# Fused soft-capped attention and spectral mixing: scores of the first channel slot in two visits, its weight splits and sums reordered, one copy moved in the first mixing slot

## The chip, the cores and the metric

The kernel runs on 1 core of one Trainium2 chip. The metric is the device time of one execution in microseconds (us). Before the change it is 856.89 us, the median of 3 runs (856.53 to 857.65).

## The reference

The kernel computes attention with a soft cap on the scores, and then a mixing stage on its output. All inputs are float32; the batch is 8, with 12 heads, 448 positions and 64 features per head, so the model width is 768.

```python
def _attn_ref(q, k, v, cap):
    scores = (1.0 / np.sqrt(q.shape[-1])) * np.matmul(q, k.transpose(0, 1, 3, 2))
    scores = cap * np.tanh(scores / cap)
    scores = scores - np.max(scores, axis=-1, keepdims=True)
    attn = np.exp(scores)
    attn = attn / (np.sum(attn, axis=-1, keepdims=True) + 1e-09)
    return np.matmul(attn, v)

def _moe_ref(x, w_theta, w_tok_r, w_tok_i, w_ch):
    theta = x @ w_theta
    zr, zi = x * np.cos(theta), x * np.sin(theta)
    y = np.einsum('ts,bsd->btd', w_tok_r, zr) + np.einsum('ts,bsd->btd', w_tok_i, zi)
    u = x + y
    return u + np.maximum(u @ w_ch, 0.0)
```

The cap is 30. The kernel holds two programs, one of them for caps above 64 (`general`); only the other one runs here.

## The kernel before

**Slots.** Attention goes in 24 slots of 4 heads (two pairs, k = 2s and 2s + 1); three slots make one batch. The mixing stage of a batch lags: slot LEAD = 4 does the theta products of batch 0, slot 5 its token mixing, slot 6 its channel products, slot 7 theta of batch 1, slot 8 its mixing, and so on in threes. So slot 6 is the first channel slot. It also splits most of the channel weights, which happens once.

**Order.** Nothing is scheduled by a planner. `pipeline` (L735) walks a script of words per slot (L704 to L733), and every word issues its instructions at once; each engine and each DMA queue works in the order in which it got them, and waits in that order. So a word's place in the script sets its place in the queue of every engine that it uses.

**The words that matter.** `S0` to `S3` are the score products of one slot (L333): S0 the first two row chunks of the first pair; S1 its third chunk and, ahead of it, the remainders of both pairs (four pairs of products, two side by side); S2 and S3 the three chunks of the second pair. `t0` to `t3` are the tanhs that read them (L384, on ScalarE), `e0` to `e3` the exps (L422), `a0a` to `a1b` the additions of the exps (L440, on VectorE). `V0`, `W`, `Vr` are the products with v of the slot before, `Rb` the sums of its exps over the rows (L491), `cV0` and `cV1` the copies of its output (L486), `I` the inversion of its sums (L538), which transposes the sums (`turn`, L526), takes the reciprocal, transposes again and sends it by four DMAs on the SP queue to the tiles bc; `N` and `N-` multiply the output by bc (L561, VectorE). `Pa1`, `Pb1`, `Pa0`, `Pb0` split the raw q and k of a pair into a high part (a cast on ScalarE at first) and a low part (VectorE) (L305, L312). `u0` to `u5`, `Xh`, `Yh`, `Yl` split the inputs of the channel and theta products the same way (L569). `C0` to `C5` are the channel products (18 products each), `c0` to `c5` their results (VectorE, then a store on SP), `T0` to `T5` the theta products.

**Channel weights.** They come as float64 words in 12 half blocks, ch0a to ch5b. `:@ch3b` loads one, by two DMAs of 384 KB on the POOL queue (L187, L188); `:*ch3b` scales it on ScalarE (L153); `:0ch3b` and `:1ch3b` are four instructions on VectorE (L197 to L201); `:2ch3b` is a cast of the high part on ScalarE (L203) and the low part on VectorE (L204). C3 needs ch3a in its first half and ch3b in its second.

**Rooms.** Tiles of the large and of the small kind live in lists of rooms (L48). A take gets the first free room, and the new tile's first writer waits for the last users of the old one. By these lists ch3b goes into the room of ch2a, ch4a into that of ch2b, ch4b into that of ch3a and ch5a into that of ch3b, before and after.

**Two forms of scores.** Slots from HALVES on have the scores of S0 and S1 in two tiles of two banks each (s0, s1), S2 and S3 in four banks that all other products share, and `once` (L284) is true for them: half tanhs, a third chunk in s1, other rooms for the second pair's split k, the sums turned directly behind their products into the first tile of S1 (L523), cV1 on VectorE (L488). Slots below HALVES have one tile of four banks that S0, S1 and S2 take in turn, and tanhs of a whole tile. Slot 6 is of the second kind before the change:

```python
HALVES = LEAD + 3                                   # L43
def once(s):                                        # L284
    return LEAD + 2 < s < NS
if k + 1 < 2 * NS:                                  # L330, in prep_k
    load_raw(k + 1, 1, k % 2 == 0 and by_scalar(k) and k > 2 * LEAD + 8)
elif word == "I":                                   # L779, in run
    if done:
        invert(k)
```

Of the kernel before, what the change touches and what calls it, by code (L numbers as in the profile page):

```python
# [28 lines left out]
LEAD = 4  # L29
# [10 lines left out]

FOLD = (0, 1, 2)

HALVES = LEAD + 3  # L43

FILL = {"branch": 10, "S0": 2, "t0": 8, "t1": 4}

# [34 lines left out]
def softcap_attn_then_spectral_mix(ctx, tc, qk2, v, cap, w_theta, w_tok, w_ch, outT):  # L81
# [9 lines left out]
    NS = B * NP2  # L91
# [190 lines left out]
            state["scores"] = state["scope"].enter_context(tc.tile_pool(name=f"ps{general}{s}", bufs=1, space=bass.MemoryType.PSUM))  # L282

    def once(s):  # L284
        return LEAD + 2 < s < NS

    def load_raw(k, part, last=False):
        t = raw[k, part] = small.take([P, S], F32, f"{'qk'[part]}{k}", None, int(part == 0 and once(k // 2) and (k // 2 - LEAD) % NP2 == 2), last)
# [23 lines left out]
    def prep_k(k, early=False):  # L312

        if 2 * WHOLE <= k < 2 * NS:
            t = raw[k, 1]
            if once(k // 2) and k % 2:
                if (k, "rooms") not in Q:
                    Q[k, "rooms"] = [small.take([P, S], F32R, f"k{k}{part}") for part in "hl"]
                rooms = iter(Q[k, "rooms"])
                Q[k, "k"] = halves(t[:, :REST], [P, REST], lambda shape, dtype, name: next(rooms)[:, :REST], f"k{k}", by_scalar(k))  # L320
            else:
                Q[k, "k"] = halves(t[:, :REST], [P, REST], lambda shape, dtype, name: wk.tile(shape, dtype, tag=f"k{name[-1]}", name=name, bufs=1), f"k{k}", by_scalar(k))
            if k % 2 == 0:
                Q[k, "r"] = wk.tile([P, S - REST], F32, tag="kr", name=f"r{k}", bufs=1)
                nc.vector.tensor_copy(Q[k, "r"], t[:, REST:])
            if early:
                Q[k, "early"] = True
            else:
                small.give(raw.pop((k, 1)))
            if k + 1 < 2 * NS:  # L330
                load_raw(k + 1, 1, k % 2 == 0 and by_scalar(k) and k > 2 * LEAD + 8)

    def scores(s, n):  # L333
        if once(s) and n >= 2:
            t = spt[s, n] = [psM.tile([P, 512], F32, tag="m", name=f"s{s}_{n}{h}") for h in range(2)]
            if n == 3:
                two = spt[s, "u"] = state["scores"].tile([P, 2, 512], F32, tag="s1", name=f"s{s}_u")
                chunk(s, (1, 2), [two[:, h] for h in range(2)])
            chunk(s, (1, n - 2), t)
        elif n == 3 and not once(s) and s not in (1, LEAD + 1):  # L340
            t = spt[s, n] = [psM.tile([P, 512], F32, tag="m", name=f"s{s}_{n}{h}") for h in range(2)]
            chunk(s, (1, 2), t)
        else:
            two = spt[s, n] = state.pop("two", None) if once(s) and n == 1 else None
            if not two:
                two = spt[s, n] = halves_of(s, n)
            for u, what in sorted(enumerate(BURSTS[n]), key=lambda at: at[1] is not None):
                chunk(s, what, [two[0][u][:, h] for h in range(2)])
        k = 2 * s + n // 2
        if n in ((1, 3) if s else (1, 2)) and s < WHOLE:  # L350
            for part in range(2):
                small.give(raw.pop((k, part)))
        elif s >= WHOLE and n % 2:
            for t in Q.pop((k, "q")) + (Q.pop((k, "rooms")) if (k, "rooms") in Q else []):
                small.give(t)
            if n == 1:
                for i in range(2):
                    small.give(raw.pop((k + i, 0)))
                if Q.pop((k + 1, "early"), False):
                    small.give(raw.pop((k + 1, 1)))  # L360
                if k + 2 < 2 * NS:
                    for i in range(2, 4):
                        load_raw(k + i, 0, once(s) and (s - LEAD) % NP2 == 2)

# [332 lines left out]
    def chan_out(b, m):  # L697
# [21 lines left out]
        " T3 Pa0 Pb0 q1 y3 e2 e3 d3 sc1 T4 y4 T5 y5 a1a a1b r2 r3 f2 f3 D1 d4 d5",  # L719
        LEAD + 1: "S0 t0 Vr V0 Ra h0a l0a h0b l0b W h1a Rb :@ch0b cV0 cV1 sc2 Pa1 S1 Pb1 q0 t1 v M0a l1a r4 h1b M0b r5 l1b f4 f5 D2 e0 h2a M1a l2a m0 :#ch0b :0ch0b e1 :1ch0b M1b h2b l2b I :2ch0b :@ch1a"  # L720
        " S2 t2 M2a h3a l3a a0a M2b h3b l3b :@ch1b m1 M3a h4a l4a :*ch1a :0ch1a M3b h4b l4b a0b e2 m2 :1ch1a S3 q1 t3 M4a h5a l5a :2ch1a :@ch2a m3 M4b"
        " h5b l5b Pa0 Pb0 :*ch1b :0ch1b a1a u0 u1 e3 :1ch1b M5a :2ch1b :@ch2b m4 u2 M5b a1b m5 u3 :*ch2a :0ch2a u4 :@ch3a",
        LEAD + 2: "S0 t0 :1ch2a :2ch2a :@ch3b V0 u5 e0 :*ch2b :0ch2b W Ra Rb Vr cV0 cV1 v :1ch2b :2ch2b :@ch4a :*ch3a :0ch3a Pa1 S1 Pb1 q0 t1 :1ch3a :2ch3a :@ch4b :*ch3b C0 I c0 :0ch3b :1ch3b a0a e1 :2ch3b :@ch5a :*ch4a C1 :0ch4a :@ch5b"
        " S2 S3 t2 :1ch4a :2ch4a :*ch4b t3 c1 :0ch4b a0b C2 :*ch5a :1ch4b :2ch4b e2 :0ch5a :*ch5b C3 c2 :1ch5a :2ch5a :0ch5b :1ch5b :2ch5b a1a Pa0 Pb0 q1 N- c3 C4 e3 a1b c4 Xh0 Xh1 Xh2 Xh3 C5 c5",
        LEAD + 3: "Pa1 S0 t0 Pb1* V0 e0 N- Yh4 Yh5 W Ra Rb Vr cV0 S1 Yl0 Yl1 Yl2 cV1 t1 S2 S3 Yl3 Yl4 Yl5 v w0 q0 I w1 a0a q1 t2 e1 a0b Pa0 Pb0 Pa3 T0 y0 t3 d0 N T1 y1 Pb3* d1 F0 sc0 T2 y2 r0 r1 f0 f1 D0"
        " T3 y3 d2 d3 e2 e3 sc1 a1a a1b F1 T4 T5 r2 r3",
        LEAD + 4: "S0 t0 y4 y5 V0 f2 W Ra Rb f3 D1 h0a h0b h1a Vr cV0 S1 cV1 d4 t1a S2 S3 t2 l0a d5 l0b I l1a sc2b M0a h1b M0b r4 l1b r5 h2a M1a t3a f4 l2a h2b f5 D2 m0 l2b M1b h3a w1 t1b N e0"
        " l3a M2a h3b l3b a0a m1 M2b e1 t3b a0b M3a h4a l4a M3b h4b l4b h5a l5a e2 m2 F0 M4a h5b a1a l5b e3 Pa0 Pb0 m3 M4b v q1 a1b M5a m4 M5b F1 w3 m5",
        NS: "u0 u1 Vr V0 u2 u3 u4 u5 W cV0 cV1 Ra Rb I C0 c0 X0 X1 C1 c1 X2 X3 C2 c2 N X4 X5 T0+ y0+ d0+ T1+ y1+ d1+ sc0+ T2+ r0+ r1+ f0+ f1+ D0+ y2+ d2+ T3+"
            " y3+ d3+ sc1+ T4+ r2+ r3+ f2+ f3+ y4+ d4+ T5+ D1+ y5+ d5+ h0a+ l0a+ h0b+ l0b+ sc2+ C3 c3 r4+ r5+ f4+ f5+ D2+ C4 h1a+ l1a+ c4 C5 c5",  # L730
# [4 lines left out]
    def pipeline(general):  # L735
        state["general"] = general
        nc.scalar.activation(curve, quarter, AF.Tanh)
        def run(s, b, word):
            if word.endswith("+"):
                b, word = b + 1, word[:-1]  # L740
# [6 lines left out]
            if word == "S0>":  # L747
                scores(s + 1, 0)
            elif name in ("S", "t", "e"):
                if live:  # L750
                    {"S": scores, "t": tanh, "e": exp}[name](s, i, *word[2:])
            elif not name:
                if live:
                    add(s, i, half)
            elif word in ("Vr^", "V0^"):
                if word == "V0^":
                    av(s, 0)
                else:
                    av_rest(s, (0,) if general else (0, 1))
                if word == "V0^" or not general:  # L760
                    used(s, word[:2])
            elif word in ("Vr", "V0", "W"):
                if done:
                    if word == "W" and ("a", k, 1) not in acc_of and k < LEAD:
                        av_rest(k, (1,))
                        used(k, "Vr")
                    if word == "Vr":
                        av_last(k) if ("a", k, 0) in acc_of else av_rest(k)
                    else:
                        av(k, 0 if word == "V0" else 1)  # L770
                    used(k, word)
            elif name == "cV":
                if done:
                    av_out(k, i)
            elif name == "R":
                if done:
                    sums(k, word)
                    used(k, word)
            elif word == "I":  # L779
                if done:  # L780
                    invert(k)
            elif word in ("N", "N-"):
                if done:
                    norm(k - len(word) + 1)
            elif word == "v":
                if live:
                    load_v(s)
            elif name == "q":
                for part in range(2):
                    if s + 1 < WHOLE or s + 1 == WHOLE and (i, part) != (1, 1):  # L790
                        load_raw(2 * s + 2 + i, part)
            elif word in ("Pa1", "Pa3"):
                prep_q(2 * s + int(word[2]))
            elif word in ("Pb1", "Pb1*", "Pb3*"):
                prep_k(2 * s + int(word[2]), "*" in word)
            elif word == "Pa0":
                prep_q(2 * s + 2)
            elif word == "Pb0":
                prep_k(2 * s + 2)
            elif name == "F":  # L800
                if live and folded(s):
                    fold(s, i)
            elif name == "w":
                weights(WEIGHTS.get((s, i), ""))
            elif name in ("u", "uh", "ul"):
                split_x(b, i, "us", name[1:] or "hl")
            elif name in ("X", "Xh"):
                if b + 1 < B:
                    split_x(b + 1, i, "xs", name[1:] or "hl")
            elif name in ("Y", "Yh", "Yl"):  # L810
                split_x(b, i, "xs", name[1:] or "hl")
            elif name in ("h", "l", "M", "sc"):
                {"h": z_high, "l": z_low, "M": mix, "sc": sincos}[name](b, i, half)
            else:
                {"T": theta, "y": turns, "d": reduce, "r": rotate, "f": flip, "D": carry, "E": carry_end, "m": mix_out, "C": chan,
                 "c": chan_out}[name](b, i)
# [73 lines left out]
```

## Time and profile before

| | |
|---|---|
| time, median of 3 | 856.89 us |
| time of the profiled execution | 856.52 us |
| its span, first to last instruction | 854.6 us |
| TensorE matmul busy | 847.7 us, 99% of the span |
| VectorE, ScalarE, GpSimd busy | 719.2, 580.3 and 116.6 us |
| granted TensorE clock, mean | 0.999 |

The profiled execution is 0.37 us under the median. Times in the trace count from the first instruction of the span. Products on TensorE overlap, so its speed is read from the distance of two starts, not from the busy time. An instruction's own duration includes an overlap with the next one too, of about a tenth of a us.

Slot 6 begins at 138.29 us with S0, slot 7 at 172.24 us, slot 8 at 205.80 us.

### The profile page before, as it was taken

How to read it: one execution, taken by the hardware profiler on the slowest of the kernel's cores; microseconds unless marked ns; L12 is line 12 of the kernel's file. 1: busy time of each engine (PE TensorE's matmuls, PEld its weight loads, DVE VectorE, ACT ScalarE, POOL GpSimd, SP SyncE). 2: the span in 40 equal slices, each digit the busy share in tenths (PEclk: the TensorE clock that was granted, in tenths of full speed). 3: DMA queues.
4: the chain of work that ended last, by engine and by line, in shares of the span. 5: the costliest groups of instructions: out<-in, count | busy, mean ns of one | idle time of the engine just before them, and what ended most of it. 6: DMA issues, size and time to landing. Idle time of an engine off the chain costs nothing.

```text
span 854.6 us, 13331 instructions
## 1 busy us (share of the span) xinstructions
PE 847.7 (99%) x4756; PEld 646.3 (76%) x4756; DVE 719.2 (84%) x1164; ACT 580.3 (68%) x736; POOL 116.6 (14%) x244
## 2 busy tenths in 40 slices
PE   9999999999999999999999999999999999999997
PEld 5335676867978779779787787797787877979996
DVE  5988979999989799879998798897988979876741
ACT  6898987789873777827867478655787377824420
POOL 1121242201300031000310013000130003200300
PEclk9999999999999999999999999999999999999999
DMA  8686275741433324322423414144142332411401
GB/s 317 197 300 229 71 233 199 261 130 43 130 90 96 97 79 117 98 97 65 131 76 97 130 58 121 50 119 130 44 130 74 99 97 63 111 44 33 141 13 57
DMA packets 51693, 99.74 MB, mean 117 GB/s; under 512 B 11233, under 2 KB 42209, under 8 KB 51617
## 3 DMA queue, kind: packets, MB, share of 16 engines
q1 hardware_dynamic: 38880, 58.81, 22.3%
q0 software_dynamic: 9568, 29.89, 11.5%
q10 hardware_dynamic: 3168, 10.09, 3.9%
q8 instruction: 39, 0.64, 0.3%
q14 instruction: 38, 0.30, 0.1%
HBM read 54.72 MB, written 11.01 MB: 77 GB/s over the span
## 4 chain that ended last, share of the span: by engine, by line
PE 96%; ACT 2%; DVE 1%; issue 0%; ACTq 0%; POOL 0%; POOLq 0%
PE s L379 13%; PE a L483 13%; PE mx L684 8%; PE mx L686 8%; PE mx L685 8%; PE th L583 7%; PE ch L583 7%; PE ch L584 7%; PE th L584 7%; PE ch L585 7%; PE th L585 7%; PE a L477 2%; PE r L521 2%; PE s_u L379 1%; ACT p L405 1%; PE fill L130 1%
## 5 line engine op out<-in xcount | busy, mean ns | idle before, releaser
L653 POOL DMA_DIRECT2D t<-g_row x160 | 78.9, 501 | 528.6 <-ACT z L607 379.0
L684 PE MATMUL mx<-wtk_h,zh 128*128 128x448 f32 x336 | 123.7, 368 | 0.0
L686 PE MATMUL mx<-wtk_h,zl 128*128 128x448 f32 x336 | 122.9, 366 | 0.1
L685 PE MATMUL mx<-wtk_l,zh 128*128 128x448 f32 x336 | 122.8, 366 | 0.0
L425 ACT ACTIVATE p<-p,singles 128x1792 f32<-128x1792 f32 (+1 forms) x76 | 117.4, 1554 | 1.6 <-PE a L483 0.6
L583 PE MATMUL th<-xs,wth_h 128*128 128x448 f32 x288 | 106.1, 368 | 0.0
L583 PE MATMUL ch<-us,wch_h 128*128 128x448 f32 x288 | 105.9, 368 | 0.0
L584 PE MATMUL ch<-us,wch_h 128*128 128x448 f32 x288 | 105.9, 368 | 0.0
L584 PE MATMUL th<-xs,wth_h 128*128 128x448 f32 x288 | 105.5, 366 | 0.0
L585 PE MATMUL th<-xs,wth_l 128*128 128x448 f32 x288 | 105.5, 366 | 0.0
L585 PE MATMUL ch<-us,wch_l 128*128 128x448 f32 x288 | 105.4, 366 | 0.0
L483 PE MATMUL a<-p,v 128*64 128x448 f32 x492 | 101.8, 545 | 0.0
L411 ACT ACTIVATE p<-s,singles 128x896 f32<-128x896 f32 x34 | 32.4, 1004 | 91.2 <-PE s L379 91.2
L483 PEld LDWEIGHTS a<-p,v 128*64 128x64 f32 x492 | 32.9, 136 | 56.5 <-issue 51.9
L684 PEld LDWEIGHTS mx<-wtk_h,zh 128*128 128x128 f32 x336 | 63.1, 188 | 9.0 <-issue 2.5
L667 ACT CAST zh<-t 128x512 fp32r<-128x512 f32 x88 | 47.3, 563 | 29.9 <-PE mx L685 13.0
L686 PEld LDWEIGHTS mx<-wtk_h,zl 128*128 128x128 f32 x336 | 63.1, 188 | 5.8 <-DVE zl L674 0.6
L685 PEld LDWEIGHTS mx<-wtk_l,zh 128*128 128x128 f32 x336 | 63.1, 188 | 5.0
L674 DVE TENSOR_TENSOR zl<-t,zh 128x512 fp32r<-128x512 f32 x88 | 52.7, 611 | 12.2 <-ACT zh L667 11.1
L583 PEld LDWEIGHTS th<-xs,wth_h 128*128 128x128 f32 x288 | 54.0, 188 | 7.8 <-ACT p L408 1.9
L583 PEld LDWEIGHTS ch<-us,wch_h 128*128 128x128 f32 x288 | 54.0, 188 | 7.1 <-ACT p L408 1.6
L584 PEld LDWEIGHTS th<-xs,wth_h 128*128 128x128 f32 x288 | 54.0, 188 | 4.9 <-DVE xs L576 0.2
(718 smaller groups left out, 1707.6 us busy)
## 6 DMA issues: line engine op xcount, KB each, us to landing
v<-in_v ACTq DMA_DIRECT2D x22, 448.0 KB, 3.8
bc<-ri SPq DMA_DIRECT2D x88, 112.0 KB, 2.8
t<-g_row SPq DMA_DIRECT2D x160, 56.0 KB, 2.4
t<-g_row POOLq DMA_DIRECT2D x160, 56.0 KB, 2.2
q<-in_qk SPq DMA_DIRECT2D x39, 224.0 KB, 3.3
k<-in_qk SPq DMA_DIRECT2D x39, 224.0 KB, 3.7
out_dram<-x SPq DMA_DIRECT2D x34, 224.0 KB, 1.9
x_row<-in_qk SPq DMA_DIRECT2D x18, 224.0 KB, 2.8
```

Source lines behind the costliest of these rows:

```text
L379: nc.tensor.matmul(out[h][rows, :S], kk[half], qq[half], start=m == 0, stop=m == len(products) - 1)
L425: nc.scalar.activation(pp, pp, AF.Exp, scale=cap_sb)
L483: nc.tensor.matmul(acc_of["a", s, i][h * D : (h + 1) * D, :S], vt[s][:, 6 * i + 3 * h + c, :], U[s, (i, c)][:, h, :], start=first and c == ...
L583: nc.tensor.matmul(acc[:, :S], wh[:, j, ms], t[:, 0, :], start=j == 0, stop=False)
L584: nc.tensor.matmul(acc[:, :S], wh[:, j, ms], t[:, 1, :], start=False, stop=False)
L585: nc.tensor.matmul(acc[:, :S], wl[:, j, ms], t[:, 0, :], start=False, stop=j == NJ - 1)
L653: queue.dma_start(t[32 * m : 32 * m + 32, d * S : (d + 1) * S], f[32 * d : 32 * d + 32, m * S : (m + 1) * S])
L667: nc.scalar.copy(zh.rearrange("p c (d x) -> p c d x", x=32), tokens(b, j)[:, c0:c1])
L674: nc.vector.tensor_tensor(zl, tokens(b, j)[:, c0:c1], zh.bitcast(F32), op=ALU.subtract)
L684: nc.tensor.matmul(acc[:, :S], zh, wtk_h[:, c, :], start=c == 0, stop=False)
L685: nc.tensor.matmul(acc[:, :S], zh, wtk_l[:, c, :], start=False, stop=False)
L686: nc.tensor.matmul(acc[:, :S], zl, wtk_h[:, c, :], start=False, stop=c == NC2 - 1)
```

## The change

The bound HALVES and `once` move from slot 7 to slot 6, so slot 6 gets the second form of scores. Its script is rewritten: S2 and S3 follow S1, so TensorE does all scores of the slot before C0 (they make up two visits with S0, around the products with v); q13 and k13 are split at the start of the slot; t1 and t2 stand ahead of the casts and scales of weights from ch2a on; the sums are inverted behind the last weight split (`I-`, in the program that runs here; the other program keeps `I^` at the old place). The first instruction word of ch2a moves from slot 5 to slot 6. The load of k14 moves from prep_k to the end of S1. In slot 8 the word `h1a`, a cast of tokens on ScalarE (L667), moves from behind `h0b` to behind `t2`.

```diff
-HALVES = LEAD + 3
+HALVES = LEAD + 2
...
     def once(s):
-        return LEAD + 2 < s < NS
+        return LEAD + 1 < s < NS
...
-            if k + 1 < 2 * NS:
+            if k + 1 < 2 * NS and k != 2 * HALVES + 1:
                 load_raw(k + 1, 1, k % 2 == 0 and by_scalar(k) and k > 2 * LEAD + 8)
...
                 if k + 2 < 2 * NS:
+                    if s == HALVES:
+                        load_raw(k + 2, 1)
                     for i in range(2, 4):
...
-        " h5b l5b Pa0 Pb0 :*ch1b :0ch1b a1a u0 u1 e3 :1ch1b M5a :2ch1b :@ch2b m4 u2 M5b a1b m5 u3 :*ch2a :0ch2a u4 :@ch3a",
-        LEAD + 2: "S0 t0 :1ch2a :2ch2a :@ch3b V0 u5 e0 :*ch2b :0ch2b W Ra Rb Vr cV0 cV1 v :1ch2b :2ch2b :@ch4a :*ch3a :0ch3a Pa1 S1 Pb1 q0 t1 :1ch3a :2ch3a :@ch4b :*ch3b C0 I c0 :0ch3b :1ch3b a0a e1 :2ch3b :@ch5a :*ch4a C1 :0ch4a :@ch5b"
-        " S2 S3 t2 :1ch4a :2ch4a :*ch4b t3 c1 :0ch4b a0b C2 :*ch5a :1ch4b :2ch4b e2 :0ch5a :*ch5b C3 c2 :1ch5a :2ch5a :0ch5b :1ch5b :2ch5b a1a Pa0 Pb0 q1 N- c3 C4 e3 a1b c4 Xh0 Xh1 Xh2 Xh3 C5 c5",
+        " h5b l5b Pa0 Pb0 :*ch1b :0ch1b a1a u0 u1 e3 :1ch1b M5a :2ch1b :@ch2b m4 u2 M5b a1b m5 u3 :*ch2a u4 :@ch3a",
+        LEAD + 2: "Pa1 S0 t0 Pb1* V0 e0 :*ch2b u5 W Ra Rb Vr cV0 S1 cV1 t1 S2 S3 t2 :0ch2a :1ch2a :2ch2a :@ch3b :0ch2b :1ch2b :*ch3a t3 :2ch2b :@ch4a v :0ch3a q0 I^ a0a e1 :1ch3a :2ch3a :@ch4b :*ch3b C0 :0ch3b c0 :1ch3b :*ch4a :2ch3b :@ch5a C1 :0ch4a :@ch5b"
+        " a0b :1ch4a :2ch4a :*ch4b c1 :0ch4b C2 :*ch5a :1ch4b :2ch4b e2 :0ch5a :*ch5b C3 c2 :1ch5a :2ch5a :0ch5b :1ch5b :2ch5b Pa0 Pb0 I- a1a q1 N- c3 C4 e3 a1b c4 Xh0 Xh1 Xh2 Xh3 C5 c5",
...
-        LEAD + 4: "S0 t0 y4 y5 V0 f2 W Ra Rb f3 D1 h0a h0b h1a Vr cV0 S1 cV1 d4 t1a S2 S3 t2 l0a d5 l0b I l1a sc2b M0a h1b M0b r4 l1b r5 h2a M1a t3a f4 l2a h2b f5 D2 m0 l2b M1b h3a w1 t1b N e0"
+        LEAD + 4: "S0 t0 y4 y5 V0 f2 W Ra Rb f3 D1 h0a h0b Vr cV0 S1 cV1 d4 t1a S2 S3 t2 h1a l0a d5 l0b I l1a sc2b M0a h1b M0b r4 l1b r5 h2a M1a t3a f4 l2a h2b f5 D2 m0 l2b M1b h3a w1 t1b N e0"
...
-            elif word == "I":
-                if done:
+            elif word in ("I", "I^", "I-"):
+                if done and (word == "I" or general == (word == "I^")):
                     invert(k)
```

## Rows read from the trace of the kernel before

**Rows 1.** The page's part 4: the chain that ended last, shares by engine.
```profile
PE 96%; ACT 2%; DVE 1%; issue 0%; ACTq 0%; POOL 0%; POOLq 0%
```
**Rows 2.** Timeline, TensorE, slot 6: start us, us long, engine, line, operation, tiles.
```profile
154.99 0.36 PE L585 MATMUL ch<-us,wch_l 128*128 128x448 f32 x1
...
155.59 0.36 PE L379 MATMUL s<-q13h,k13l 64*128 64x448 f32 x2
...
157.01 0.39 PE L379 MATMUL s<-q13l,k13h 64*128 64x448 f32 x2
...
157.63 0.37 PE L584 MATMUL ch<-us,wch_h 128*128 128x448 f32 x1
```
**Rows 3.** Timeline, TensorE, slot 8: the end of S2 and the begin of S3.
```profile
214.75 0.37 PE L379 MATMUL s<-q17h,k17l 64*128 64x448 f32 x2
215.20 0.47 PE L379 MATMUL s_u<-q17h,k17h 64*128 64x448 f32 x2
```
**Rows 4.** Timeline, ScalarE, slot 8: token casts and the first half of t1.
```profile
212.26 1.55 ACT L667 CAST zh<-t 128x512 fp32r<-128x512 f32 x3
...
214.14 1.01 ACT L411 ACTIVATE g_row<-s,singles 128x896 f32<-128x896 f32 x1
```
**Rows 5.** Timeline, VectorE, slots 6 and 7; in brackets the idle time before and its releaser.
```profile
147.54 0.36 DVE L197 TENSOR_SCALAR g_row<-g_row 128x384 int32<-128x384 int32 x1 [0.88 <-ACT g_row L153]
...
151.04 0.60 DVE L299 TENSOR_TENSOR q13l<-q,q13h 128x448 fp32r<-128x448 f32 x1
...
152.04 0.35 DVE L201 TENSOR_SCALAR swc3a<-swc3a 128x384 int32<-128x384 int32 x1
...
152.90 0.64 DVE L529 STREAM_TRANSPOSE ri<-r 128x448 f32<-128x448 f32 x1
153.58 0.24 DVE L552 RECIPROCAL folds<-ri 128x14 f32<-128x14 f32 x1
...
154.42 0.58 DVE L700 SCALAR_TENSOR_TENSOR x<-ch,x 128x448 f32<-128x448 f32 x1
...
157.45 0.55 DVE L204 SCALAR_TENSOR_TENSOR wch_l<-swc3b 128x384 fp32r<-128x384 uint32 x1
...
167.80 0.35 DVE L197 TENSOR_SCALAR swc5b<-swc5b 128x384 int32<-128x384 int32 x1
...
169.93 1.08 DVE L445 TENSOR_TENSOR ps<-p 128x896 f32<-128x896 f32 x1
...
177.95 0.62 DVE L564 TENSOR_TENSOR x_row<-bc,x_row 128x448 f32<-128x448 f32 x1
```
**Rows 6.** Timeline, ScalarE, slots 6 and 7: an exp, a cast of xs, half tanhs.
```profile
152.87 1.78 ACT L425 ACTIVATE g_row<-g_row,singles 128x1792 f32<-128x1792 f32 x1
...
178.60 0.57 ACT L574 CAST xs<-x_row 128x448 fp32r<-128x448 f32 x1 [0.45 <-DVE x_row L564]
...
181.01 1.01 ACT L411 ACTIVATE p<-s,singles 128x896 f32<-128x896 f32 x1 [0.25 <-PE s L379]
...
181.91 1.00 ACT L411 ACTIVATE p<-s,singles 128x896 f32<-128x896 f32 x1
```
**Rows 7.** Timeline, POOL queue, slot 6: the loads of ch3b and ch5a.
```profile
146.79 0.54 POOL L187 DMA_DIRECT2D swc3b<-in_wch  x1 [4.74 <-DVE us L576]
...
158.66 0.54 POOL L187 DMA_DIRECT2D swc5a<-in_wch  x1 [3.92 <-ACT p L405]
```
**Rows 8.** DMA issues, 120 to 180 us: tiles, queue, KB each, median us to landing.
```profile
g_row<-in_wch POOLq DMA_DIRECT2D x3, 384.0 KB, 4.9
...
swc2a<-in_wch POOLq DMA_DIRECT2D x1, 384.0 KB, 3.8
...
swc4b<-in_wch POOLq DMA_DIRECT2D x1, 384.0 KB, 6.6
```
**Rows 9.** Timeline, TensorE: S1's last chunk in slot 6, T0 in slot 7.
```profile
146.93 0.47 PE L379 MATMUL s<-q12h,k12h 64*128 64x448 f32 x2
...
183.52 0.47 PE L583 MATMUL th<-xs,wth_h 128*128 128x448 f32 x1
```

## The prediction, made before the change was run

> **What bounds the kernel now.** The chain that ended last comes first: TensorE holds 96% of it, ScalarE 2%, VectorE 1% [rows 1]. So only what makes TensorE start its next product later or earlier can move the time. I then read TensorE's timeline from 100 us on, looking for steps from one start to the next that are longer than the usual one. The usual step is 0.203 us: seven of them lie between 155.59 and 157.01 [rows 2]. Two kinds of longer step touch the change: the border between 64-row score products and 128-row products, in slot 6, and one real wait in slot 8 [rows 3]. After that I read ScalarE, VectorE, the POOL queue and the landing times through slots 6 and 7, because the change rewrites their order and TensorE's orders all wait on them. The sum is made against the profiled execution, 856.5 us, which is 0.4 below the median 856.9; I add the difference to the median.
>
> **Slot 6: one visit instead of two (gain 0.41).** Before, S2 and S3 stand between C1 and C2. Going in takes 0.60 from 154.99 to 155.59, coming out 0.62 from 157.01 to 157.63, each where two usual steps would be 0.41 [rows 2]. That is 1.22 against 0.81: 0.41 us. With S2 and S3 directly behind S1 no border is left there, and the number of products stays the same. C0 to C5 then stand in a row and each of C2 to C5, and all of slot 7, falls due 0.41 earlier.
>
> **Slot 8: the copy h1a (gain 0.25).** In slot 8 TensorE waits once: from 214.75 to 215.20, 0.45 for a step of 0.20 [rows 3]. The products that start at 215.20 reuse the bank that the tanh at 214.14 reads, and that tanh ends at 215.15. It starts late because three casts, 1.55 us from 212.26, stand ahead of it [rows 4]. Without h1a, some 0.5 of it, the tanh can follow the S1 products that feed it by 0.4 sooner; 0.25 is all there is to win. Behind t2 the cast is still ahead of its user M1a, which stands 21 products (4.3 us) behind the start of the mixing products, and is hidden; it pushes sc2b back by 0.5, and with it the rotation, transposition and transfer of the last token group, which M4a needs 84 products (17 us) behind that start. It costs nothing while that distance holds. Bounds: 0 and 0.25.
>
> **Slot 6: what else moves, engine by engine.** Steps: an instruction on ScalarE starts 0.11 before the end of the one ahead (1.01 long, the next 0.90 later [rows 6]). So half a tanh costs 0.90, a cast or scale 0.46 (0.57 long), an exp 1.70 (1.78 long) [rows 6]; a tanh of one head 0.52. One half block of w_ch costs VectorE 2.13 (167.80 to 169.93, five instructions) [rows 5].
>
> VectorE. Before, at 147.54 it begins ch2b, after 0.88 idle [rows 5]; ch2a is then done. Now the low parts of us, q13 and k13, the turn of the sums and cV1 (a copy of 0.54 that ScalarE did) come ahead of ch2a. cV1 writes into the room of q12, which is free when S1's first four pairs end, at 147.0: the next pair starts at 146.93 [rows 9], the last of the four some 0.5 before. So cV1 ends, and ch2a begins, at 147.6: 0.06 later than ch2b before. From there VectorE owes ch2a in addition (+2.13) and no longer the low parts of q13 and k13 (1.00, from 151.04 to 152.04) nor turn, reciprocal and second transposition (1.52, from 152.90 to 154.42) [rows 5]. The last two of these (0.84, from 153.58) come back behind the last weight split, ahead of slot 7. So the first product x*bc of slot 7, at 177.95 before [rows 5], would come at 177.95 + 0.06 + 2.13 - 2.52 + 0.84 = 178.46 if VectorE never waited.
>
> SP queue. The four bc transfers leave their place behind the second transposition (154.42 [rows 5]) for the end of the slot. With the wait worked out below that transposition would end near 172.9, 6.8 us ahead of the product that needs bc; hidden unless the four take that long to issue and land. k14's load moves behind S1, to about 148, some 20 us ahead of its split. Hidden.
>
> The weight loads. ch3b needs ch2a's room, and ch2a's cast now stands behind t1 and t2. t1 starts at 147.1, two halves 1.80, t2 two heads 1.04, the cast 0.46: its end is 150.5. POOL starts a load 0.65 after the last user of its room has ended (158.66 against 157.45 + 0.55) [rows 5, 7]. So ch3b is issued at 151.15; before it was at 146.79 [rows 7]. ScalarE meanwhile does the scale of ch3a, t3, a cast, e1, a cast and is free for ch3b's scale at 155.4. VectorE, with three half blocks and one addition (1.0) behind 147.6, is ready for ch3b at 155.0. With a landing of L the scale ends at 151.15 + L + 0.5, so VectorE waits L - 3.35, and never less than 0.9, because of ScalarE. ch4a is issued at 154.0 by the same rule; its block waits another 0.2, if both loads take L.
>
> L: the trace shows 3.8 for ch2a, which had the queues nearly to itself, 4.9 as the median of three, and 6.6 for ch4b, which shared them with bc [rows 8]. In the new order fewer loads overlap and bc is gone; v and the second halves still run beside. I take 4.4, midway between the first two, and keep 3.8 and 6.6 as ends. Wait on VectorE: 1.25 (ends 0.9 and 3.45).
>
> **What that does to slot 7.** The product comes at 178.46 + 1.25 = 179.71. The casts of xs follow it by 0.65 (178.60 after 177.95), a second by 0.53, then cV0; t1 starts 2.1 behind the product: 181.8. Before it was at 181.01, where ScalarE waited for TensorE [rows 5, 6]. The theta products start 2.51 behind t1's start (183.52 against 181.01) [rows 6, 9], since their bank is read by t2: 184.3, 0.8 later than before. Without any wait on VectorE t1 could start at 180.55, and 180.60 is what TensorE asks for once the 0.41 is gained: the whole gain hangs on this wait. In slot 6 itself C5 would wait some tenths for the cast of ch5a; that is inside the 0.8, since slot 7 waits longer. Sum: +0.8 - 0.25 = +0.5 on the profiled execution: 857.0; on the median, **857.4**. Ends: with 0.9 of waiting +0.4 - 0.25 = +0.2; with 3.45 +3.0 - 0.25 = +2.7.
>
> A lateness of VectorE beyond slot 7's theta should not cost again: slot 7 leaves VectorE waiting for TensorE's theta results, and slot 8 for the sums.
>
> **Rivals.** *The gain comes through whole.* If t3 or e1 is out of the way sooner than I count, or VectorE makes up the wait before 177, TensorE keeps 0.41 + 0.25: 856.2. For it: without a wait the chain is in time by 0.05, and VectorE's own work shrinks in the slot. Against: ScalarE's fixed order makes 0.9 of waiting even with a fast load. Chance 0.22.
>
> *Loads land sooner.* With L at 3.8 or under, the wait is ScalarE's 0.9 alone: +0.2, 857.1. For it: ch2a's row; against: v and the second halves run beside. Chance 0.12. The Trainium skill, page "DMA: Bandwidth & Descriptors", section "Anatomy of one DMA", speaks for this case: it gives a load from POOL as about 2.0 us plus its bytes over 436 GB/s, an estimated 2.9 us for 384 KB. The landing rows stand against that rule: the shortest is 3.8.
>
> *Slower: loads land late.* One mechanism: ch3b, ch4a and then ch5a queue behind each other's second halves and v, each waits for a cast that waits for the load before, and TensorE stands at C4 and C5 and again in slot 7. At 6.6 us [rows 8] this is +2.7: 859.6. It decides from about L = 5.6, where VectorE waits 2.45 and the sum passes 1.7. For it: loads under way together took up to 6.6. Against: bc, whose small packets ran beside that one, is gone. Chance 0.16.
>
> *The change doesn't do what it says.* S3 could wait behind t1's first half, in slot 6 as it does in slot 8, and give a border's worth back; then about +0.9: 857.8. In slot 7, with the same order, it doesn't. Chance 0.08.
>
> **How the numbers follow.** A measurement of this kernel tells 0.2%, 1.7 us, from no change. My case has 0.42: 857.4, its own range 856.6 to 858.3. Faster by 1.7 is out of reach, as only 0.66 is on offer; 0.03 for what I don't see. Slower by 1.7 is the late-load case, 0.16, and 0.01 of others: 0.17. Within: 0.80. The range, from 856.1 (whole gain) to 858.8 (L near 5.7), leaves out some 2 in 10, most of it above.
>
> **What would show it.** Right: S2 and S3 follow S1 with no step over 0.3 between; no score products between C1 and C2; VectorE idle about 1.0 to 1.5 ahead of ch3b's first instruction, ended by ScalarE's scale; ch3b's load issued near 151; the first product of slot 7 near 179.7; theta at 184.3; in slot 8 no step of 0.45. Wrong: no idle on VectorE in 150 to 160 with theta near 183.1 (whole gain), or steps of half a us and more inside C4 and C5 (late loads), or a new wait behind sc2b in slot 8.

## The result, and the profile after

The changed kernel takes **863.46 us** (median of 6 runs, 862.21 to 864.62); the kernel before took 856.74 us (6 runs) on the same chip. The ratio is 1.0077, 95% interval 1.0067 to 1.0088: slower by about 6.7 us, where +0.5 was forecast and the range ended at 858.8. The profiled execution has a span of 861.7 us against 854.6, and its mean granted clock is 0.997 against 0.999.

First the chain that ended last, on the page of the changed kernel (compare [rows 1]):

```profile
PE 92%; DVE 2%; ACT 2%; DMA 2%; SPq 1%; issue 1%; ACTq 0%; POOL 0%; DVEq 0%; POOLq 0%
```

TensorE falls from 96% to 92% of the chain, and DMA and SP's queue, which had no share before, now hold 3%. The same chain in order of time, from 168 to 192 us (start, us long, what), shows where:

```profile
171.96 0.66 DVE ri L555
...
172.63 0.47 SPq L559
...
174.60 0.54 SPq L559
...
175.18 2.28 DMA bc<-ri
...
177.59 1.09 DVE ps L447
...
179.13 0.62 DVE x L566
179.75 0.54 DVE x_row L702
...
180.34 3.92 PE a L485 x12
```

Read it from below. TensorE's second v products of slot 7 (`W`) start at 180.34, behind the result c3 (L702), which stands on VectorE behind a product (L566) and the addition `a1a` (L447). And a1a waits for the four transfers of the inverted sums, `bc<-ri`: issued from 172.63 on, the last landing at 177.46. VectorE's timeline in slots 6 and 7 (in brackets the idle time before and its releaser; compare [rows 5]):

```profile
147.52 0.35 DVE L197 TENSOR_SCALAR swc2a<-swc2a 128x384 int32<-128x384 int32 x1
...
156.10 0.40 DVE L197 TENSOR_SCALAR swc3b<-swc3b 128x384 int32<-128x384 int32 x1 [1.11 <-ACT swc3b L153]
...
171.69 0.23 DVE L554 RECIPROCAL folds<-ri 128x14 f32<-128x14 f32 x1
171.96 0.65 DVE L555 STREAM_TRANSPOSE ri<-folds 128x448 f32<-128x448 f32 x1
177.59 1.09 DVE L447 TENSOR_TENSOR ps<-p 128x896 f32<-128x896 f32 x1 [4.98 <-DMA bc<-ri]
...
184.51 0.61 DVE L566 TENSOR_TENSOR x<-bc,x 128x448 f32<-128x448 f32 x1
...
185.58 0.64 DVE L531 STREAM_TRANSPOSE ri<-s 128x448 f32<-128x448 f32 x1
```

The row at 177.59 is the new one: **4.98 us of idle time**. a1a does not read bc. It *writes* a tile of the kind `ps`, of which there are two in turn, and the turned sums `ri` are such a tile as well. Since the sums are now turned directly behind their products, the turn is: ri, then the tile of a0a, then that of a1a, which is ri's buffer again. The transfers read that buffer until 177.46. Before, the same two names shared it too, but a1a came at 169.93 [rows 5] and the transfers had left from 154.53 on (SP's queue before):

```profile
154.53 2.40 SPq L557 DMA_DIRECT2D bc<-ri  x4
```

On TensorE (start, us long, line, operation, tiles; compare [rows 2, 3, 9]):

```profile
149.22 0.37 PE L381 MATMUL s<-q13h,k13l 64*128 64x448 f32 x2
149.53 0.47 PE L585 MATMUL ch<-us,wch_h 128*128 128x448 f32 x1
...
180.34 2.51 PE L485 MATMUL a<-p,v 128*64 128x448 f32 x6 [4.10 <-DVE x_row L702]
...
186.74 0.47 PE L381 MATMUL s<-q14h,k14h 64*128 64x448 f32 x2
...
189.38 0.47 PE L585 MATMUL th<-xs,wth_h 128*128 128x448 f32 x1
...
220.61 0.37 PE L381 MATMUL s<-q17h,k17l 64*128 64x448 f32 x2
220.81 0.40 PE L381 MATMUL s_u<-q17h,k17h 64*128 64x448 f32 x2
```

S3 runs into C0 with one border (149.22 to 149.53), as forecast. T0, the first theta product, starts at 189.38 instead of 183.52 [rows 9]: +5.86. In slot 8 the step of 0.45 [rows 3] is gone (220.61 to 220.81). From starts like these come the lengths of the stretches that the change touches. Slot 6, from its S0 to the S0 of slot 7: 33.94 before, 34.10 after. Slot 7 up to T0: 11.28 and 17.04. Slot 8 up to its first mixing product: 10.81 and 10.49. Sum: +0.16 + 5.76 - 0.32 = +5.6 us. The rest of the 7.1 between the spans is in the mixing products, which the change doesn't touch (last section). In a second trace of the changed kernel the three stretches take 34.44, 17.91 and 10.49, together +6.8 us.

The windows around the wait (the stretch and its length, the busy us of PE, PEld, DVE, ACT and POOL with the number of instructions, the granted clock, the share of the DMA engines and GB/s):

```profile
175.69:180.34 4.65, 0.55 (x5) 0.01 (x1) 2.75 (x5) 1.05 (x3) 0.00 (x0) 0.95 0.23 51
180.34:183.34 3.00, 3.00 (x10) 1.01 (x12) 2.94 (x4) 3.00 (x6) 0.00 (x0) 0.51 0.21 76
183.34:186.00 2.66, 2.66 (x26) 0.78 (x26) 2.66 (x6) 2.21 (x3) 0.00 (x0) 1.00 0.77 234
```

TensorE's step at the wait is 4.65 where 0.37 is usual: 4.3 us lost (the 4.10 of the row counts only from the end of the product ahead). The granted clock falls while TensorE still stands (its mean in that stretch is 0.95). Then, from 180.34 to 183.34, the granted clock is 0.51, the lower of its two levels (1.2 instead of 2.4 GHz), and four steps take 0.70 to 0.80.

### The profile page after: what moved, and what is told of

It reads as the page before. It is cut to its first block, busy times and chain, and to the rows that moved or that the text cites. A ratio compares the mean times of both kernels' runs of the same rounds, so it can differ in the third digit from the quotient of the medians.

```text
span 861.7 us, 13329 instructions
## 1 busy us (share of the span) xinstructions
PE 850.5 (99%) x4756; PEld 646.3 (75%) x4756; DVE 719.8 (84%) x1165; ACT 580.9 (67%) x739; POOL 117.0 (14%) x244
## 4 chain that ended last, share of the span: by engine, by line
PE 92%; DVE 2%; ACT 2%; DMA 2%; SPq 1%; issue 1%; ACTq 0%; POOL 0%; DVEq 0%; POOLq 0%
PE a L485 13%; PE s L381 12%; PE mx L686 7%; PE mx L688 7%; PE mx L687 7%; PE th L585 7%; PE th L586 7%; PE th L587 7%; PE ch L585 6%; PE ch L587 6%; PE ch L586 6%; PE a L479 2%; PE r L523 2%; PE s_u L381 1%; SPq L655 1%
## 5 line engine op out<-in xcount | busy, mean ns | idle before, releaser
L413 ACT ACTIVATE p<-s,singles 128x896 f32<-128x896 f32 x36 | 34.3, 1004 | 91.4 <-PE s L381 91.3
L585 PEld LDWEIGHTS th<-xs,wth_h 128*128 128x128 f32 x288 | 54.0, 188 | 7.7 <-ACT p L410 1.9
L587 PEld LDWEIGHTS ch<-us,wch_l 128*128 128x128 f32 x288 | 54.0, 188 | 5.5 <-DVE wch_l L204 0.7
```

Of the source, the lines that this page charges most:

```text
L585: nc.tensor.matmul(acc[:, :S], wh[:, j, ms], t[:, 0, :], start=j == 0, stop=False)
L587: nc.tensor.matmul(acc[:, :S], wl[:, j, ms], t[:, 0, :], start=False, stop=j == NJ - 1)
```

## The experiments

**Theories.** A: a1a takes ri's buffer and waits for the bc transfers; everything else of the loss follows. B: the weight loads and casts come late and keep VectorE behind. C: the bc transfers land late, and whoever *reads* bc waits. D, for the half clock: it comes from TensorE's idle time and adds to the loss. The sum of A and D on TensorE alone would be 4.3 + 1.5 = 5.8.

**The inverted sums in a tile of their own**, everything else as in the change:

```diff
+        own = s == HALVES - 1 and not state["general"]
+        if own:
+            ri = small.take([P, S], F32, f"ro{s}")
         nc.vector.transpose(out=ri, in_=few.unsqueeze(2).broadcast_to([P, S // 32, 32]))
...
-        if direct(s) and not state["general"]:
+        if direct(s) and not state["general"] or own:
             small.give(ri)
```

> The changed kernel, except that the second transposition of slot 5's sums writes into a small room of its own instead of back into the tile that the first one filled; place and time of the inversion stay. Theory A (the addition a1a takes the buffer of the turned sums, because the two buffers of that kind go round, and so waits until the four bc transfers have read it): the 5.0 us wait of VectorE ahead of a1a is gone, the first product x*bc of slot 7 comes near 179.3, the theta products start near 183.9 instead of 189.4, TensorE keeps its full clock in slot 7; time 858.0. Theory B (the late weight loads and casts keep VectorE behind, and a1a only shows it): a1a starts no sooner than 176, time about 863. Theory C (the transfers land late, and whoever needs bc waits): the wait moves to the product x*bc in slot 7, time 860 to 862.

Measured: 857.95 us, ratio 1.0005 (0.9995 to 1.0015). VectorE's timeline in this run:

```profile
172.04 0.65 DVE L558 STREAM_TRANSPOSE ro<-folds 128x448 f32<-128x448 f32 x1
172.60 1.05 DVE L447 TENSOR_TENSOR ps<-p 128x896 f32<-128x896 f32 x1
...
179.49 0.62 DVE L569 TENSOR_TENSOR x<-bc,x 128x448 f32<-128x448 f32 x1
...
180.56 0.65 DVE L531 STREAM_TRANSPOSE ri<-s 128x448 f32<-128x448 f32 x1
```

and T0 on TensorE's:

```profile
184.17 0.47 PE L588 MATMUL th<-xs,wth_h 128*128 128x448 f32 x1
```

a1a follows the transposition at once, although the transfers leave when they did. With one buffer more, the whole loss but some tenths is gone: A holds. C falls, because the first product with the slot's bc (179.49) waits for nothing. B is left with what this kernel still lacks: T0 at 184.17 is 0.65 later than before.

**The inversion earlier**: back ahead of a0a, or ahead of the last weight block only (fragments of the script):

```diff
-q0 I^ a0a e1
+q0 I a0a e1
-Pa0 Pb0 I- a1a q1
+Pa0 Pb0 a1a q1
```

> The changed kernel with the inversion of the sums back ahead of a0a, where the other program keeps it; all else stays, the two visits, the half tanhs and the late casts. Theory A: the transfers are read out some 10 us before a1a, no wait on them; the 0.84 us of reciprocal and transposition fall into the 1.1 us that VectorE waits for ch3b, so the chain to slot 7 is shorter than in the run with a tile of its own: theta near 183.2, time 856.0 to 856.9, at or a little under the kernel before. Theory B: the weight chain is as late as before, 862 to 863.

```diff
-:1ch5a :2ch5a :0ch5b
+:1ch5a :2ch5a I- :0ch5b
-Pa0 Pb0 I- a1a q1
+Pa0 Pb0 a1a q1
```

> The changed kernel with the inversion one half block earlier, between the last steps of ch5a and the first of ch5b, 3.2 us sooner. Theory A: the wait ahead of a1a is the landing less a1a's readiness, so it falls from 5.0 to about 1.8; TensorE's wait ahead of the second v products falls from 4.3 to about 1, the stretch at half clock behind it is gone; time 859 to 860. Theory B: no change, 863. Theory C: as A at most by the 3.2 us.

Measured: ahead of a0a 858.84 us, ratio 1.0011 (1.0000 to 1.0023), slot 7 again 11.28 up to T0, without a wait. The expected gain over the kernel before (856.0 to 856.9 us) didn't show in the time, which came out a little above it; in the trace the three stretches are together 0.31 shorter. Where the rest of the time lies no trace shows. Ahead of ch5b 859.3 us, ratio 1.0020 (1.0009 to 1.0031), with a short wait on VectorE:

```profile
169.21 0.65 DVE L555 STREAM_TRANSPOSE ri<-folds 128x448 f32<-128x448 f32 x1
...
174.12 1.09 DVE L447 TENSOR_TENSOR ps<-p 128x896 f32<-128x896 f32 x1 [1.06 <-DMA bc<-ri]
```

Between the transposition and a1a now stand 3.3 us of other work (to 173.06), and a1a waits 1.06 instead of 4.98. So the distance from the inversion to a1a sets the wait. It isn't all that this place costs: the inversion now stands ahead of the split of ch5b, TensorE waits 0.55 us in C5 for the cast of ch5b (a step of 0.92 at 171.33), and slot 6 takes 35.17 instead of 34.10.

**The copy in slot 8 alone**, on the kernel before:

```diff
-h0a h0b h1a Vr cV0 S1 cV1 d4 t1a S2 S3 t2 l0a
+h0a h0b Vr cV0 S1 cV1 d4 t1a S2 S3 t2 h1a l0a
```

> The kernel before with nothing but the copy h1a of slot 8 behind t2. All theories: the one step of 0.45 us at the begin of S3 in slot 8 goes back to about 0.2; gain 0.25 to 0.3, time 856.4 to 856.5, and nothing new behind it in slot 8.

Measured: 857.4 us, ratio 0.9996 (0.9986 to 1.0006); slot 8 up to mixing takes 10.50 instead of 10.81. In the trace the gain is there, in the time it can't be told from none.

**What stands behind a1a: c3 ahead of it.**

```diff
-Pa0 Pb0 I- a1a q1 N- c3 C4 e3
+Pa0 Pb0 I- c3 a1a q1 N- C4 e3
```

> As the changed kernel, with c3 (the result of C3) ahead of I's successor a1a on VectorE. It takes apart what stands behind the waiting addition. If it is c3's place behind a1a that holds TensorE (its second v products W need the bank that c3 reads), then W runs on at 175.7 without a wait; a1a still waits some 4.3 us for the bc transfers (c3 takes 0.6 of the 4.98), and TensorE then stands at the sums Rb, which need a1b: a1b would end near 181.4, so TensorE waits about 3.3 us there instead of 4.27, T0 comes near 186.7 instead of 189.38, and the time is about 2.5 us under the changed kernel, some 861 us. If TensorE was held by something else (the transfers themselves or the casts), W still waits near 175.7 for over 4 us. On the clock: a wait of over 3 us with half clock behind it again (0.5) would speak for the idle time as its cause; if the clock stays at 1.0, the stop of over 4 us or its place matters.

Measured: 861.86 us, ratio 1.0062 (1.0048 to 1.0075). The waits of TensorE from 174 to 188 us:

```profile
PE s L523 <- ACT g_row L413: 2.8, 1, 2.8
PE s L381 <- DVE ri L531: 1.2, 1, 1.2
```

W no longer waits, so it was c3's place that stopped TensorE at 175.7. But TensorE goes only 2 us further: it then waits 3.0 us (a step of 3.38) at the sums, whose bank the tanh t0 still reads, and t0 stands behind casts of xs that need a product which is queued behind a1a; and again at S1 for the turn of the sums (L531). I expected T0 near 186.7; it came at 188.05, because I had named a1b as the next holder and not t0, and had left out the turn.

**The half clock.** The unchanged change once more, then three fillings of the wait with ten useless products of 0.37 us, added to the work. First into the bank of the sums (e6), then into the second tile of S1 (e8). The cut shown is e6's; e8 has `[0][1]` where it has `[0][0]`, and a line that hands `two` on to the sums is left out:

```diff
                         av(k, 0 if word == "V0" else 1)
+                    if word == "V0" and s == HALVES + 1 and not general:
+                        state["two"] = halves_of(s, 1)
+                        r = state["two"][0][0][:, 0]
+                        for n in range(10):
+                            rows = slice(n % 2 * D, (n % 2 + 1) * D)
+                            nc.tensor.matmul(r[rows, :S], vt[k][:, n // 2, :], U[k, (0, n // 2 % 3)][:, n % 2, :], start=True, stop=True)
```

> The changed kernel as it is, on the same chip as the three others, for its time and a second execution's trace. If the half clock belongs to the wait and not to one execution, it is there again: a wait of 4.2 to 4.4 us at 175.7, granted clock near 0.5 for some 3 us behind it, T0 near 189.4, ratio 1.0067 to 1.0088.

> As the changed kernel, with ten useless products (the first v products over again, results into the bank of the sums, overwritten later) put behind V0 of slot 7, where TensorE stands idle for 4.27 us. Nothing else waits less. If the half granted clock at 180.3 to 183.4 comes from the idle time, it is 1.0 there now, the steps of the second v products are 0.37 instead of 0.70 to 0.80, and T0 comes about 1.5 us sooner than in the changed kernel, near 187.9: more work and about 1.5 us less time, some 862 us where the changed kernel takes 863.5. If the slow steps come from something else (the place, VectorE's reads of the banks, the transfers), they stay 0.70 to 0.80, T0 stays at 189.4 and the time at 863.5.

> As e6_filled_wait, but the ten useless products write the second tile of S1, which nobody reads at that time, instead of the bank that t0 reads; so they can start at once, and TensorE is idle for 4.27 - 3.73 = 0.5 us instead of 4.27. Everything else as in the changed kernel: c3 ends near 180.3 and the second v products start there. If the half granted clock comes from the idle time ahead of it, it stays at 1.0, the v products' steps are 0.37 instead of 0.74, T0 comes near 187.9 instead of 189.4 to 190.5, and the time is some 1.5 to 2.4 us under the changed kernel's (862.8 on this chip's last runs): ratio near 1.0045 to 1.005. If the place or VectorE makes the slow steps, they stay at 0.74 and T0 at 189.4 or later, ratio 1.0067 or more.

Measured: 862.78 us for the change again (ratio 1.0067, 1.0054 to 1.0081), 869.05 (1.0142, 1.0126 to 1.0157) and 870.72 us (1.0159, 1.0146 to 1.0173) for the two fillings. Both missed, and for one reason: t0 reads *both* tiles of S0, which S1 takes over, so the useless products waited for t0 themselves (steps of 5.9 and 6.6 us) and pushed everything behind them. They don't fill the wait, they lengthen it. The third filling uses V0's own bank, ahead of V0:

```diff
         first = av_room(s, i)
+        if s == HALVES and i == 0 and not state["general"]:
+            for n in range(10):
+                h = n % 2
+                nc.tensor.matmul(acc_of["a", s, i][h * D : (h + 1) * D, :S], vt[s][:, 3 * h + n // 2 % NC, :], U[s, (i, n // 2 % NC)][:, h, :], start=True, stop=True)
```

> As the changed kernel, with ten useless products (0.37 each) in slot 7 ahead of V0 and into V0's own bank, which V0 then overwrites. That bank is free at that time, so they start at 173.8 without a wait (in e6 and e8 they had to wait for t0, which reads both score tiles). TensorE then ends V0 near 179.6 and is idle for only some 0.6 us before c3 frees the bank of W near 180.5. If the half granted clock comes from the idle time ahead of it, it stays at 1.0, W's steps are 0.37, and T0 comes 1.5 to 2.4 us sooner than in the changed kernel's two traces, near 188.0: the time 1.5 to 2.4 us under it, ratio near 1.0045 to 1.005. If something else makes the slow steps, they stay at 0.74, T0 at 189.4 to 190.5 and the ratio at 1.0067 to 1.0077.

Measured: 864.54 us, ratio 1.0082 (1.0069 to 1.0096). Windows of four runs follow, in each the stretch of the wait (in the last one, of the work that fills it) and the one behind it, with the columns as above. The change again:

```profile
175.99:180.63 4.64, 0.55 (x5) 0.01 (x2) 2.76 (x5) 1.05 (x3) 0.00 (x0) 0.78 0.23 51
180.63:185.32 4.69, 4.69 (x15) 1.25 (x15) 4.62 (x7) 4.36 (x6) 0.00 (x0) 0.50 0.37 136
```

The second filling:

```profile
176.59:183.23 6.64, 0.55 (x6) 0.01 (x2) 5.03 (x7) 3.39 (x6) 0.00 (x0) 0.79 0.22 61
183.23:187.50 4.27, 4.27 (x13) 1.47 (x14) 2.98 (x6) 3.12 (x4) 0.00 (x0) 0.53 0.68 225
```

The run with c3 first:

```profile
177.78:181.16 3.38, 0.54 (x4) 0.00 (x0) 3.35 (x5) 2.48 (x5) 0.00 (x0) 1.00 0.00 0
181.16:185.15 3.99, 2.77 (x26) 0.81 (x26) 3.96 (x9) 3.99 (x6) 0.00 (x0) 1.00 0.58 182
```

The third filling, from its first useless product on:

```profile
174.66:180.34 5.68, 5.68 (x33) 2.20 (x32) 1.95 (x3) 0.24 (x1) 0.00 (x0) 1.00 0.37 80
180.34:183.57 3.23, 2.97 (x19) 0.79 (x16) 3.17 (x5) 3.23 (x6) 0.00 (x0) 1.00 0.19 71
```

In these traces the half clock stands behind the stops of 4.3 us and of 6.3 (and of 5.6 in the first filling, 0.52 behind it), not behind that of 3.0. The last is one execution: its mean granted clock over the span is 0.999, but the other four of that run have 0.996 or 0.997, as the first six of the changed kernel have, while none of the kernel before is under 0.998. So the clock very likely fell in those four too; where, no trace shows, and the stop of 3.0 tells nothing about a length that would be harmless. The half clock is gone where the useless products keep TensorE busy through the same wait of VectorE (4.90 us at a1a in that run): 1.00 in the trace, a mean of 0.999 in all five executions. The place and VectorE's wait are the same there and TensorE's idle time is gone, so the idle time is the cause. But the time didn't fall, and this is the second half of the answer: with the clock at 1.00, TensorE reached S1's third chunk sooner and stood there for the turn of the sums, which VectorE does ten rows behind a1a. VectorE in the third filling:

```profile
186.38 0.64 DVE L535 STREAM_TRANSPOSE ri<-s 128x448 f32<-128x448 f32 x1
```

and TensorE there:

```profile
187.08 0.47 PE L381 MATMUL s<-q14h,k14h 64*128 64x448 f32 x2 [0.91 <-DVE ri L535]
...
190.00 0.47 PE L589 MATMUL th<-xs,wth_h 128*128 128x448 f32 x1
```

The chunk starts 0.70 behind the turn's start, and T0 3.62 behind it; in the run with the own tile 3.61 as well. In the changed kernel the chunk starts at 186.74, 1.16 behind the turn at 185.58. So the half clock cost 1.16 - 0.70 = 0.46 at the chunk, not 1.5, and the rest of it ran beside VectorE's queue (by the same working 1.3 in the second trace, where the turn itself waited 0.44 for TensorE). At T0 less is left of it, since T0 follows the chunk by 2.92 with the clock kept and by 2.64 in the changed kernel. Slot 7 up to T0 is 16.77 with the clock kept, 17.04 and 17.91 in the two traces of the change: 0.27 and 1.14. D holds for the cause and falls for the size. By the stretches the third filling is 5.3 us behind the kernel before, by its time 7.0 (5.9 to 8.2); that its time is not under the change's is in part left open.

**The casts and loads forward**, on top of the own tile: ch2a's first words go ahead of the low parts of q13, its cast (`:3`) behind e0 and its low part (`:4`) behind the turn, where the one word `:2` did both; the load of ch3b follows. ch2b's and ch3a's casts and ch3b's scale move one place forward on ScalarE (fragments of slots 5 and 6; `uh4` and `ul4` are the cast and the low part of u4):

```diff
-m5 u3 :*ch2a u4 :@ch3a
+m5 u3 :*ch2a uh4 :0ch2a :1ch2a :@ch3a
-V0 e0 :*ch2b u5 W Ra Rb Vr cV0 S1 cV1 t1 S2 S3 t2 :0ch2a :1ch2a :2ch2a :@ch3b :0ch2b :1ch2b :*ch3a t3 :2ch2b :@ch4a v :0ch3a q0 I^ a0a e1 :1ch3a :2ch3a :@ch4b :*ch3b C0
+V0 e0 :3ch2a :*ch2b uh5 W Ra Rb :4ch2a :@ch3b Vr cV0 S1 cV1 ul4 ul5 t1 S2 S3 t2 :0ch2b :1ch2b :*ch3a :2ch2b :@ch4a t3 v :0ch3a q0 I^ a0a :3ch3a :*ch3b e1 :1ch3a :4ch3a :@ch4b C0
```

> As e2_own_tile (the inverted sums in a tile of their own), and the weight chain brought forward: ch2a's first words ahead of the low parts of q13, its cast behind e0 and its low part behind the turn of the sums, so ch3b's load is issued near 148.0 instead of 150.9; ch2b's and ch3a's casts and ch3b's scale one place sooner on ScalarE; the low parts of the last two us behind cV1. VectorE's wait ahead of ch3b (1.08 in e2) should be gone and VectorE some 1.5 to 1.9 sooner at ch5b. Then C4 and C5 wait for no cast (0.5 us in e2) and S1 of slot 7 not for its half tanh (0.46): T0 near 183.2 instead of 184.17, span some 0.6 below the kernel before, time ratio 0.9990 to 0.9996 where e2 stood at 1.0005. If the loads then only meet each other (theory: late transfers), a wait of 0.5 to 1 us appears ahead of ch4a or ch4b instead and the ratio stays near 1.0005.

Measured: 856.55 us (11 runs) against 856.70 (15 runs) before, ratio 0.9999 (0.9990 to 1.0008). The POOL queue in this run:

```profile
147.96 0.54 POOL L187 DMA_DIRECT2D swc3b<-in_wch  x1 [5.59 <-DVE x_row L491]
```

VectorE:

```profile
154.24 0.36 DVE L197 TENSOR_SCALAR swc3b<-swc3b 128x384 int32<-128x384 int32 x1
...
157.65 0.36 DVE L197 TENSOR_SCALAR g_row<-g_row 128x384 int32<-128x384 int32 x1 [0.58 <-ACT g_row L153]
```

and T0 on TensorE:

```profile
183.38 0.47 PE L589 MATMUL th<-xs,wth_h 128*128 128x448 f32 x1
```

The wait ahead of ch3b is gone, 0.58 of it comes back ahead of ch4a, and C0 to C5, slot 7 and slot 8 have no wait left: slot 6 33.57, slot 7 11.27, slot 8 10.49, together 0.70 us less than before, and 0.98 less than with the own tile alone. The 0.98 is what B was worth, and the 0.70 the whole of what the change could give. In the time it is not to be told from the kernel before: no version here beats that one measurably.

## Why the prediction was wrong

**The step that failed** is the SP queue's: "With the wait worked out below that transposition would end near 172.9, 6.8 us ahead of the product that needs bc; hidden unless the four take that long to issue and land." The transposition ended at 172.61 and the four took 4.85 us, so by this sentence all was hidden. It asked who *reads* what the transfers write, and not who next *writes* what they read. That is a1a, directly behind the transposition on VectorE. It became so by two parts of the change together: `I-` put the inversion directly ahead of a1a, and the second form of scores turns the sums, and so takes ri, ahead of a0a, with the inversion far behind.

**From 4.98 us of a wait to 5.76 us of loss.** I had VectorE due just in time for slot 7, 0.05 ahead without any wait, and that was right: hence every us at a1a counted, by three paths that the runs showed (c3 to W's bank, xs to t0 to the bank of the sums, the turn to S1). Slot 7 up to T0 takes the loss apart: 11.28 before, 11.75 with the own tile (+0.47, the lateness of VectorE that was forecast), 16.77 with the wait but the clock kept (+5.02 for 4.90 us at a1a), 17.04 in the change (+0.27 for the half clock). That 4.3 + 1.5 on TensorE alone also comes to 5.8 is chance. The text said that a lateness of VectorE beyond slot 7's theta would not cost again; slot 8 began its products on time, so that stands.

**What was right.** ch2a began at 147.52 (147.6 forecast). ch3b's load left at 150.84 (151.15), took 4.6 us (L = 4.4), and VectorE waited 1.11 ahead of ch3b (1.25). POOL's loads in the changed kernel (KB each, median us to landing; compare [rows 8]):

```profile
swc3b<-in_wch POOLq DMA_DIRECT2D x1, 384.0 KB, 4.6
swc5a<-in_wch POOLq DMA_DIRECT2D x1, 384.0 KB, 4.0
```

The rule of the Trainium skill, page "DMA: Bandwidth & Descriptors", section "Anatomy of one DMA", which I had cited for loads that land sooner, makes an estimated 2.9 us of each of these; the rows again stand above it. The product of slot 7 was forecast at 179.71 and theta at 184.3; the run with the own tile has 179.49 and 184.17, and the changed kernel's 184.51 is the forecast plus 4.80. C5 waited 0.54 ("some tenths"), which used up the border's 0.41 in slot 6; but it waited for the low parts of ch5a and ch5b on VectorE (L204, ending at 168.55 and 170.67), not for the cast that I had named. Slot 8 gave 0.32 (0.25 forecast).

**The rivals.** The slower one, late loads, had the right sign and the wrong place: the loads took about what I had taken, and TensorE stood at no weight split for more than some tenths. Nor were the bc transfers slow. With almost nothing beside them they were quicker than before. Issues of the kernel before from 154 to 158 us, then of the changed one from 172 to 176:

```profile
bc<-ri SPq DMA_DIRECT2D x4, 112.0 KB, 6.3
```

```profile
bc<-ri SPq DMA_DIRECT2D x4, 112.0 KB, 2.5
```

Missing was a rival in which the inversion's transfers hold not only their target but their source.

## What to carry to other kernels

When a step that ends in transfers is moved, list two things: who reads what they fill, and who next takes the buffer that they read from. In a pair of rotating tiles the second one may be the very next instruction on the same engine, and then the whole latency of the transfers lies on that engine's queue. One look at the order of takes of that tile kind answers it, and a tile of its own removed it here, with some tenths of a us left over (ratio 1.0005, 0.9995 to 1.0015).

When a wait opens on TensorE, follow the waiting engine's queue to its end before adding up: freeing the first victim moved the stop by 2 us only, and of the 1.5 us that the slower clock seemed to cost, only 0.27 counted in that trace; the rest was spent beside that queue.

## What the runs showed of the hardware that was not expected

The granted clock fell to its lower level in one single stop of TensorE of 4.3 us, before TensorE went on (mean 0.95 and 0.78 in the stretch of the stop). It then stayed there for 3.0 us in one execution and 4.7 in another of the same kernel, while TensorE worked without a gap. So the same stop cost 0.27 and 1.14 us in two executions.

The 126 mixing products of a slot take 25.40 or 26.23 us without a wait in either case: the steps are 0.20 or 0.21. Other slots lie between or up to 26.66, where the two rates mix or single steps are longer. It changes between two executions of one kernel. Slot 11 in the changed kernel's two traces, first mixing product and first product behind them:

```profile
323.76 0.48 PE L686 MATMUL mx<-wtk_h,zh 128*128 128x448 f32 x1
...
349.98 0.47 PE L381 MATMUL s<-q24h,k24h 64*128 64x448 f32 x2
```

```profile
325.01 0.47 PE L686 MATMUL mx<-wtk_h,zh 128*128 128x448 f32 x1
...
350.42 0.47 PE L381 MATMUL s<-q24h,k24h 64*128 64x448 f32 x2
```

26.22 against 25.41. Over the seven slots with mixing from slot 8 on, the profiled executions of this study add up to between 180.5 (the change again) and 182.7 us (the first filling), with 180.6 for the kernel before and 182.0 for the changed one. So a difference of spans of 1 to 2 us between two single traces of this kernel says nothing unless it is found in the stretches that were changed; why the products step in two rates was not tried.
